# A buffer of its own for the fourth head output at the fourth place, and one left-over product moved, in a recurrent-memory transformer kernel

## The chip, the cores and the metric

The kernel runs on one core of a Trainium2 chip. Times are device microseconds (us) of one launch. A core has a matrix engine (PE in the profile; PEld is its weight load), a vector engine (DVE), a scalar engine (ACT), GpSimd (POOL), and SyncE (SP), which here only issues transfers (DMA). Each engine works through its own list in order and waits on semaphores that others raise.

## The reference

The input `x` has 2048 rows of 640. It is cut into 64 segments of 32 rows. A memory of 8 rows is put in front of each segment; attention with 32 heads of 192 runs over these 40 rows; its first 8 output rows are the memory of the next segment. So segment s+1 can't begin before the output product of segment s.

```python
for s in range(n_seg):                      # 64 segments, one after the other
    xs = x[:, s * seg_len:(s + 1) * seg_len, :].copy()
    h = jnp.concatenate([mem, xs], axis=1)  # 8 + 32 rows
    q = jnp.einsum('btd,dhe->bhte', h, Wq)
    k = jnp.einsum('btd,dhe->bhte', h, Wk)
    v = jnp.einsum('btd,dhe->bhte', h, Wv)
    scores = jnp.einsum('bhqe,bhke->bhqk', q, k) * scale
    scores = jnp.where(mask[None, None], scores, -1000000000.0)
    p = _softmax(scores, axis=-1)
    o = jnp.einsum('bhqk,bhke->bhqe', p, v)
    o = jnp.einsum('bhte,hed->btd', o, Wo)
    mem = o[:, :M, :].copy()                # M = 8
    outs.append(o[:, M:, :])
```

The result is mixed with a gated feed-forward block of the same `x` by a sigmoid gate, row by row. The feed-forward block is done once, ahead of the segments.

## The kernel before

**Layout of the work.** After the feed-forward block, `segment(s)` is recorded 64 times. The 32 heads are four *octets* of eight heads; the places of the four octets in a segment are called i = 0 to 3. Segments go in groups of four, and the *place* of a segment is q = s % 4, so there are places 0, 1, 2 and 3 (place 3 is the "fourth place" of the change). Of each segment's 32 rows, 24 are done with the memory rows in the segment itself. The other 8 are the *left rows*: four segments' left rows make 32 rows, and their Q, K and V products are done together, ahead of time. Only place 3 finishes the left rows' attention output: there the output product runs over 64 rows (40 of the segment, 24 left rows of the three segments ahead) and is a function of its own, `wo_both`; places 0 to 2 use `wo_part`.

**The order.** The order of the steps in a segment is a table written by hand: `PROG` for places 0 and 2, `PROG1` (the same but for one step) for place 1, `PROG3` for place 3. Each engine's list follows the table; a recording layer (`_Sched`) adds the waits from the regions that each step reads and writes. The steps:

- `("g", n, k)`: product of 128 of the 640 inputs for group n of Q, K or V of some octet (L1134, and L226 where the stationary operand is kept). The last k of a group is followed by the copy of the product out of PSUM: L1155 for Q and K, L1158 for V, both on ACT.
- `tq`, `tk`: DVE turns Q and K (L1172). `sc`: scores (L1183 to L1198 on PE). `ex`: softmax. `pt`: the probabilities are turned on PE (L1245, L1250).
- `("pv", i)`: probabilities times V of octet i, the *head outputs* (L1278 and L1280 on PE), written to SBUF by ACT (L1300 or L1310) and DVE (L1304 or L1315). At place 3 POOL also puts the left rows' head outputs beside them (L1292).
- `("wo", i, h)`: half h of octet i's output product. Place 3: L1372, 12 matmuls for a half, gathered in one PSUM bank. Places 0 to 2: L1328, and L1354 for octet i = 3.
- `("lf", q, u, k)`: step k of the left rows' Q and K product of the next group, done at place q only (L926 and L226). `le` takes it out (L1400, L1402).
- `("vb", k)`: at place 3, step k of the left rows' V product for the next group, five steps of four matmuls (L967). Nothing in its own segment reads it.

**The end of a segment at place 3.** After the last `wo`, DVE and ACT copy the memory rows out of PSUM (L1561, L1564), DVE turns them into the next segment's input (L1572, two pieces), and `("g", 0, 0)` of the next segment starts on the first piece. DVE then adds the segment's rows to the output (L1083, L1431).

**Buffers.** At place 3 the head outputs of every octet go into `U3`, one buffer of 4 x 3 x 64 values per partition. So `pv` of an octet can be written only after both halves of `wo` of the octet ahead have read it. At places 0 to 2 there are two buffers, and octet i = 3 is written in two halves with regions of their own.

**Weights.** Most of the weights stay in SBUF. 16 pieces share their space with another piece; after such a piece is used, SP loads its partner into the space in the same segment (L631). At place 3 three pieces of Wo are loaded so after `("wo", 0, 0)` and `("wo", 0, 1)` and used in `("wo", 3, 0)` and `("wo", 3, 1)`, in the order in which they are loaded.

Of the kernel before, what the change touches and what calls it, by code (L numbers as in the profile page):

```python
# [238 lines left out]
def _build(nc, A_x, A_mem0, A_Wq, A_Wk, A_Wv, A_Wo, seg_len, w_gate, w_up, w_down,  # L239
           gate_w, out, opts=None):  # L240
# [9 lines left out]
    DJ = Dm // 4  # L250
    NT = H // 2
    NPAIR = NT // 2
    NOCT = NT // 4
# [4 lines left out]
    R = L + M  # L258
# [15 lines left out]
    S_ = _Sched(nc)  # L274
# [18 lines left out]
    wsB = {}  # L293
# [43 lines left out]
    ps = nc.alloc_psum_tensor("ps", [128, 8, 512], F32)  # L337
# [3 lines left out]
    o = wsA_base - wsB_total  # L341
    assert o == w_cap
    wsB_off = {}
# [4 lines left out]
    o = wsA_base  # L348
# [4 lines left out]
    o = ffn_base  # L353
# [73 lines left out]
    U3 = bview(wsB_off["uT"], 1536).rearrange("p (t c r) -> p t c r", c=3, r=64)  # L427
    r_U3 = sreg(wsB_off["uT"], 1536)
    r_U3p = [[sreg(wsB_off["uT"] + x + 4 * i, 4) for x in (0, UB)] for i in range(3)]
    st_f = [[fview(wsA_off["stats"] + (2 * b + i) * 16, 16) for i in (0, 0, 1)] for b in range(2)]  # L430
    r_st = [sreg(wsA_off["stats"] + 32 * b, 32) for b in range(2)]
    uTl = bview(wsB_off["uTl"], NCH * XA * 2).rearrange("p (c t) -> p c t", t=XA)
# [85 lines left out]
    def piece_view(key, o):  # L518
        if key[0] == 3:
# [17 lines left out]
    PROG3 = [("g", 0, 0), ("g", 0, 1), ("g", 0, 2), ("g", 0, 3), ("g", 0, 4), ("tq", 0), ("g", 1, 0), ("tk", 0),  # L537
# [58 lines left out]
    o = 0  # L596
# [496 lines left out]
    LB = 4  # L1093
# [15 lines left out]
    def apx(ap, dims):  # L1109
        return bass.AP(ap.tensor, ap.offset, [list(ap.ap[0])] + [list(d) for d in dims])  # L1110
# [155 lines left out]
    def pv_oct(s, o):  # L1266
# [20 lines left out]
        S_.add("pe", fns, reads=[r_v[o % NVB], r_vl[oc], r_PT], writes=[r_ps[A]] + ([r_ps[B]] if B != A else []), name="PVa s%d o%d" % (s, o))  # L1287
        na = 2 if o in USPLIT else 3
        q = s % 4
        if q == 3:  # L1290
            u, ru = U3, r_U3p
            S_.add("pool", lambda e: e.tensor_copy(  # L1292
                out=U3.rearrange("p t c r -> p (t c) r")[:, :, R:64], in_=uTl[:, 12 * oc:12 * oc + 12, :]),
                reads=[r_uTl[oc]], writes=r_U3p[2], name="U3l s%d o%d" % (s, o))
        if o == NOCT - 2 and s + 1 < NSEG:
            ek_copy(s, (3,))
        if o == NOCT - 1 and q < 3:
            assert na == 2 and o % NUB == 1 and WOP == 4
            for h in ((0, 1), (1, 0))[s % 2]:
                S_.add("act", lambda e, h=h: e.activation(  # L1300
                    out=apx(u[:, 2 * h, 0, :], [[R, 2], [3 * R, 2], [1, R]]),
                    in_=ps[:, A, 0:2 * W].rearrange("p (c t r) -> p c t r", t=4, r=R)[:, :, 2 * h:2 * h + 2], func=ACTF.Copy),
                    reads=[r_ps[A]], writes=[r_uThp[h][0]], name="uT evac s%d o%d" % (s, o))
                S_.add("dve", lambda e, h=h: e.tensor_copy(  # L1304
                    out=u[:, 2 * h:2 * h + 2, 2, 0:R],
                    in_=ps[:, B, 2 * W:3 * W].rearrange("p (t r) -> p t r", r=R)[:, 2 * h:2 * h + 2]),
                    reads=[r_ps[B]], writes=[r_uThp[h][1]], name="uT mid s%d o%d" % (s, o))
        else:
            rs = R if q < 3 else 64
            S_.add("act", lambda e: e.activation(  # L1310
                out=apx(u[:, 0, 0, :], [[rs, na], [3 * rs, 4], [1, R]]),
                in_=ps[:, A, 0:na * W].rearrange("p (c t r) -> p c t r", t=4, r=R), func=ACTF.Copy),
                reads=[r_ps[A]], writes=ru[0] if na == 2 else ru[0] + ru[1], name="uT evac s%d o%d" % (s, o))
            if na == 2:
                S_.add("dve", lambda e: e.tensor_copy(out=u[:, :, 2, 0:R], in_=ps[:, B, 2 * W:3 * W].rearrange("p (t r) -> p t r", r=R)),  # L1315
                       reads=[r_ps[B]], writes=ru[1], name="uT mid s%d o%d" % (s, o))
# [51 lines left out]
    def wo_both(s, item):  # L1368
        for p in wo_pairs(s, item):
            g_, rg_ = piece(s, (3, p))  # L1370
            for c in range(3):
                S_.add("pe", [lambda e, i=i, g_=g_, c=c, p=p: e.matmul(  # L1372
                    ps[64 * i:64 * i + 64, LB, 0:2 * DJ], U3[:, p % 4, c, :], g_[:, c, 2 * DJ * i:2 * DJ * (i + 1)],
                    start=(p == NWP - 1 and c == 0), stop=(p == 0 and c == 2), tile_position=(0, 64 * i),
                    skip_group_check=True) for i in range(2)],
                    reads=[rg_, r_U3], writes=[r_ps[LB]], name="Wb s%d p%d" % (s, p))

    late_at = ("g", 1, KT - 1)
    r_lsth = [sreg(lst_off[3] + 768 * m, 768) for m in range(2)]
# [1 line left out]
    for x, prog in enumerate(PROGS):  # L1381
        at = prog.index
        g_end = {mi: at(("g", n, KT - 1)) for n, ms in enumerate(GROUPS) for mi in ms}
        assert g_end[(2, 1)] < at(("wo", 0, 0))
        assert at(("sc", 2)) < at(("pv", 1))
        assert all(at(("wo", i, 1)) < at(("pv", i + (1 if x == 3 else 2))) for i in range(NOCT - (1 if x == 3 else 2)))
# [279 lines left out]
```

## Time and profile before

| | |
|---|---|
| median of 3 runs | 1659.49 us (1658.9 to 1665.99) |
| profiled execution, own time | 1669.24 us |
| its span, first to last instruction | 1667.5 us |
| granted PE clock, mean | 0.996 |
| busy share of the span: PE, PEld | 94%, 47% |
| busy share: DVE, ACT, POOL | 60%, 47%, 33% |
| DMA: read and written | 473.25 MB, 21.09 MB |

A row of a timeline gives the start (us from the span's start), how long the row lasted, the engine, the line, and in brackets how long the engine stood idle before it and what ended that wait. A row "A <- B: total, times, longest" of the waits is idle time of engine A that B ended. Matmuls are pipelined and their ends are modelled, so starts are compared with starts where it matters.

### The profile page before, as it was taken

How to read it: one execution, taken by the hardware profiler on the slowest of the kernel's cores; microseconds unless marked ns; L12 is line 12 of the kernel's file. 1: busy time of each engine (PE TensorE's matmuls, PEld its weight loads, DVE VectorE, ACT ScalarE, POOL GpSimd, SP SyncE). 2: the span in 40 equal slices, each digit the busy share in tenths (PEclk: the TensorE clock that was granted, in tenths of full speed). 3: DMA queues.
4: the chain of work that ended last, by engine and by line, in shares of the span. 5: the costliest groups of instructions: out<-in, count | busy, mean ns of one | idle time of the engine just before them, and what ended most of it. 6: DMA issues, size and time to landing. Idle time of an engine off the chain costs nothing.

```text
span 1667.5 us, 75813 instructions
## 1 busy us (share of the span) xinstructions
PE 1566.5 (94%) x37107; PEld 779.2 (47%) x28147; DVE 1000.1 (60%) x3023; ACT 785.5 (47%) x1874; POOL 549.9 (33%) x1609
## 2 busy tenths in 40 slices
PE   9999899999999999999999999999999999999986
PEld 4444345444444445444455444454444454444533
DVE  6453566656566666666565666566665656656653
ACT  2222454545555454545455554455454555545442
POOL 1110233333333333333333333333333333333332
PEclk9999999999999999999999999999999999999999
DMA  9915899888889898988889898889888898888984
GB/s 297 340 43 160 323 321 330 301 282 310 324 317 325 300 319 290 334 306 311 303 305 343 315 327 289 303 315 340 308 302 310 308 336 311 307 297 308 324 312 179
DMA packets 275415, 499.28 MB, mean 299 GB/s; under 512 B 121119, under 2 KB 136327, under 8 KB 275079
## 3 DMA queue, kind: packets, MB, share of 16 engines
q1 hardware_dynamic: 271000, 491.30, 84.2%
q8 instruction: 255, 4.18, 1.0%
q10 hardware_dynamic: 4079, 3.14, 0.6%
q14 instruction: 81, 0.66, 0.1%
HBM read 473.25 MB, written 21.09 MB: 296 GB/s over the span
## 4 chain that ended last, share of the span: by engine, by line
PE 71%; DMA 17%; DVE 6%; ACT 3%; issue 3%; SPq 1%; POOL 0%; DVEq 0%; ACTq 0%; POOLq 0%
PE ps L1134 19%; PE ps L226 17%; DMA arena<-in_A_Wv_dram 9%; PE ps L1372 7%; DMA arena<-in_A_Wo_dram 6%; PE ps L1328 5%; PE ps L1278 3%; PE ps L835 3%; PE ps L832 3%; PE ps L1354 2%; PE ps L1183 2%; PE ps L926 2%; PE ps L858 2%; PE ps L1191 1%; DMA arena<-in_A_Wk_dram 1%
## 5 line engine op out<-in xcount | busy, mean ns | idle before, releaser
L1134 PE MATMUL ps<-arena 128*32 128x384 bf16 x8640 | 645.6, 328 | 28.0 <-DVE arena L1572 11.6
L226 PE MATMUL ps<-arena 128*32 128x384 bf16 x8960 | 639.7, 326 | 2.7 <-ACT arena L1155 1.2
L1134 PEld LDWEIGHTS ps<-arena 128*32 128x32 bf16 x8640 | 231.9, 96 | 399.2 <-issue 258.9
L1172 DVE STREAM_TRANSPOSE arena<-arena 128x384 bf16<-128x384 bf16 x512 | 273.6, 559 | 70.5 <-ACT arena L1155 69.3
L1155 ACT ACTIVATE arena<-ps 128x384 bf16<-128x384 f32 x512 | 230.4, 493 | 99.0 <-PE ps L1134 93.8
L1328 PE MATMUL ps<-arena 128*32 128x320 bf16 x3456 | 184.4, 300 | 16.2 <-issue 11.1
L1175 POOL COPY arena<-arena 64x160 bf16<-64x160 bf16 x256 | 81.9, 320 | 334.3 <-DVE arena L1172 332.8
L1210 DVE TENSOR_REDUCE arena<-ps 104x4 f32<-104x160 f32 x256 | 82.9, 324 | 162.3 <-PE ps L1198 162.0
L1158 ACT ACTIVATE arena<-ps 128x384 bf16<-128x384 f32 x256 | 124.9, 488 | 88.2 <-PE ps L1134 88.2
L1263 ACT ACTIVATE arena<-ps 128x448 bf16<-128x448 f32 x192 | 104.4, 544 | 125.3 <-PE ps L1250 125.3
L1222 ACT ACTIVATE ps<-ps 104x160 f32<-104x160 f32 x256 | 74.8, 292 | 177.0 <-DVE ps L1212 175.2
L1310 ACT ACTIVATE arena<-ps 128x480 bf16<-128x480 f32 (+1 forms) x208 | 116.7, 561 | 87.4 <-PE ps L1280 86.1
L1008 POOL COPY arena<-arena 128x96 bf16<-128x96 bf16 x256 | 70.2, 274 | 246.7 <-PE ps L1198 174.4
L1224 DVE TENSOR_REDUCE arena<-ps 104x4 f32<-104x160 f32 x256 | 82.9, 324 | 83.8 <-ACT ps L1222 82.4
L1372 PE MATMUL ps<-arena 128*64 128x320 bf16 x1536 | 122.6, 307 | 0.5 <-ACT arena L1310 0.5
L1278 PE MATMUL ps<-arena 128*64 128x160 bf16 x1536 | 116.9, 240 | 5.6 <-ACT arena L1155 3.4
L1328 PEld LDWEIGHTS ps<-arena 128*32 128x32 bf16 x3456 | 89.6, 96 | 62.2 <-issue 19.1
L926 PE MATMUL ps<-arena 128*32 128x384 bf16 x1280 | 109.6, 328 | 1.1 <-issue 0.8
L1280 PE MATMUL ps<-arena 128*64 128x64 bf16 x1536 | 103.7, 193 | 2.3 <-issue 1.9
L1400 ACT ACTIVATE arena<-ps 128x384 bf16<-128x384 f32 x120 | 57.3, 490 | 101.2 <-PE ps L926 48.9
L1318 POOL COPY arena<-arena 128x96 bf16<-128x96 bf16 x192 | 51.7, 270 | 159.8 <-ACT arena L1300 88.7
L1278 PEld LDWEIGHTS ps<-arena 128*64 128x64 bf16 x1536 | 81.2, 109 | 37.6 <-ACT arena L1158 14.4
(102 smaller groups left out, 2362.6 us busy)
## 6 DMA issues: line engine op xcount, KB each, us to landing
arena<-in_A_Wk_dram SPq DMA_DIRECT2D x335, 384.0 KB, 6.5
arena<-in_A_Wv_dram SPq DMA_DIRECT2D x335, 384.0 KB, 8.7
arena<-in_A_Wo_dram SPq DMA_DIRECT2D x205, 480.0 KB, 6.0
arena<-in_A_Wq_dram SPq DMA_DIRECT2D x209, 384.0 KB, 5.5
arena<-left_qk_scratch SPq DMA_DIRECT2D x126, 96.0 KB
left_qk_scratch<-arena SPq DMA_DIRECT2D x49, 192.0 KB, 5.4
left_qk_scratch<-arena SPq DMA_DIRECT2D x30, 96.0 KB, 5.5
ffn_b_scratch<-arena ACTq DMA_DIRECT2D x16, 160.0 KB, 4.1
```

The source lines that it names most:

```text
L226: return e.add_instruction(mybir.InstMatmult(name=nm, start_tensor_calc=like["start"], stop_tensor_calc=stop, tile_size=(128, 32), tile_po ...
L926: fns.append(lambda e, outp=outp, rhs=rhs, j=j: e.matmul(outp, lhs, rhs, start=(k == 0), stop=(k == KT - 1), tile_position=(0, 32 * j)))
L1134: fns.append(lambda e, outp=outp, rhs=rhs, j=j: e.matmul(outp, lhs, rhs, start=(k == 0), stop=(k == KT - 1), tile_position=(0, 32 * j)))
L1155: S_.add("act", lambda e, m=m, bk=bk: e.activation(out=rows_sb[m], in_=ps[:, bk, 0:384], func=ACTF.Copy), reads=[r_ps[bk]], writes=[r_rows ...
L1158: S_.add("act", lambda e, i=i, bk=bk: e.activation(out=v_sb[i % NVB].rearrange("p (c n) -> p c n", c=3), in_=ps[:, bk, 0:384].rearrange("p ...
L1172: S_.add("dve", lambda e: e.transpose(out=dst[:, :, 0:L], in_=rows_sb[m].rearrange("p (c r) -> p c r", r=L)), reads=[r_rows[m]], writes=[r ...
L1263: S_.add("act", lambda e: e.activation(out=PT, in_=ps[:, bank, 0:PTW + 128], func=ACTF.Copy), reads=[r_ps[bank]], writes=[r_PT], name="pT ...
L1278: return [lambda e: e.matmul(full, v[:, e0:e0 + 64], PTm[:, i], start=True, stop=False, tile_position=(0, 64 * i), skip_group_check=True), ...
L1280: lambda e: e.matmul(part, vl[:, e0:e0 + 64], PTl[:, i], start=False, stop=True, tile_position=(0, 64 * i), skip_group_check=True)]
L1310: S_.add("act", lambda e: e.activation(out=apx(u[:, 0, 0, :], [[rs, na], [3 * rs, 4], [1, R]]), in_=ps[:, A, 0:na * W].rearrange("p (c t r ...
L1328: fns.append(lambda e, i=i, t=t, j=j, gv=gv: e.matmul(ps[32 * j:32 * j + 32, bank, 0:2 * DJ].rearrange("p (h n) -> p h n", h=2), lhs2[i], ...
L1372: S_.add("pe", [lambda e, i=i, g_=g_, c=c, p=p: e.matmul(ps[64 * i:64 * i + 64, LB, 0:2 * DJ], U3[:, p % 4, c, :], g_[:, c, 2 * DJ * i:2 * ...
```

## The change

At place 3, octet i = 3 gets buffers of its own: `U3h`, two halves laid over Q and over the probabilities, which are free by then. It is written in two halves, as at places 0 to 2. `PROG3` has another order at its end. In `PROG` (and so in `PROG1`) the step `("lf", 1, 1, 2)`, done at place 1 only, goes from ahead of `("pt", 2)` to behind `("pv", 3)`.

```diff
+    U3h = [bview(wsB_off[nm], 768).rearrange("p (t c r) -> p t c r", c=3, r=64) for nm in ("Q", "p")]
+    r_U3h = [sreg(wsB_off[nm], 768) for nm in ("Q", "p")]
...
-            ("g", 4, 3), ("le", 1, 0, 1), ("g", 4, 4), ("g", 5, 0), ("g", 5, 1), ("lf", 1, 1, 2), ("pt", 2),
+            ("g", 4, 3), ("le", 1, 0, 1), ("g", 4, 4), ("g", 5, 0), ("g", 5, 1), ("pt", 2), ("wo", 0, 1), ("tk", 3),
...
+            ("wo", 2, 0), ("pt", 3), ("wo", 2, 1), ("pv", 3), ("lf", 1, 1, 2), ("lf", 2, 1, 2), ("lf", 0, 1, 1),
...
-            ("g", 5, 4), ("wo", 2, 0), ("wo", 2, 1), ("pv", 3), ("vb", 0), ("vb", 1), ("vb", 2), ("wo", 3, 0),
-            ("wo", 3, 1), ("vb", 3), ("vb", 4)]
+            ("g", 5, 4), ("wo", 2, 0), ("pv", 3), ("wo", 2, 1), ("wo", 3, 0), ("wo", 3, 1), ("vb", 0), ("vb", 1),
+            ("vb", 2), ("vb", 3), ("vb", 4)]
...
-        if q == 3:
+        if q == 3 and o < NOCT - 1:
             u, ru = U3, r_U3p
...
+        if q == 3 and o == NOCT - 1:
+            for h in ((0, 1), (1, 0))[s % 2]:
+                S_.add("pool", lambda e, h=h: e.tensor_copy(
+                    out=U3h[h].rearrange("p t c r -> p (t c) r")[:, :, R:64], in_=uTl[:, 12 * oc + 6 * h:12 * oc + 6 * h + 6, :]),
+                    reads=[r_uTl[oc]], writes=r_U3hp[h][2], name="U3l s%d o%d" % (s, o))
...
-        if o == NOCT - 1 and q < 3:
+        if o == NOCT - 1:
             assert na == 2 and o % NUB == 1 and WOP == 4
+            uh, rh, rs = ([u[:, 2 * h:2 * h + 2] for h in range(2)], [[[x] for x in y] for y in r_uThp], R) if q < 3 else (U3h, r_U3hp, 64)
...
+            u, ru = (U3h[p % 4 // 2][:, p % 2], r_U3h[p % 4 // 2]) if item[1] == NOCT - 1 else (U3[:, p % 4], r_U3)
...
-                    reads=[rg_, r_U3], writes=[r_ps[LB]], name="Wb s%d p%d" % (s, p))
+                    reads=[rg_, ru], writes=[r_ps[LB]], name="Wb s%d p%d" % (s, p))
```

Lines move down in the changed file: L967 is L971 there, L1134 is L1138, L1278 is L1282, L1280 is L1284, L1354 is L1364, L1372 is L1383.

PE at the end of a segment at place 3, before: the output products of octets 1 and 2 end (L1372 x24 is both halves of octet 2), then the head outputs of octet 3 (L1278, L1280), then three steps of the left V product (L967).

```order
L1134 MATMUL ps<-arena 32x384 x4
L1372 MATMUL ps<-arena 64x320 x24
L1278 MATMUL ps<-arena 64x160 x2
L1280 MATMUL ps<-arena 64x4x16 x2
L1278 MATMUL ps<-arena 64x160 x2
L1280 MATMUL ps<-arena 64x4x16 x2
L1278 MATMUL ps<-arena 64x160 x2
L1280 MATMUL ps<-arena 64x4x16 x2
L967 MATMUL ps<-arena 32x384 x12
L1372 MATMUL ps<-arena 64x320 x24
L967 MATMUL ps<-arena 32x384 x8
L1134 MATMUL ps<-arena 32x384 x4
```

The same place on PE in the changed program, up to the next segment's first product (the last row):

```order
L1138 MATMUL ps<-arena 32x384 x4
L1383 MATMUL ps<-arena 64x320 x12
L1282 MATMUL ps<-arena 64x160 x2
L1284 MATMUL ps<-arena 64x4x16 x2
L1282 MATMUL ps<-arena 64x160 x2
L1284 MATMUL ps<-arena 64x4x16 x2
L1282 MATMUL ps<-arena 64x160 x2
L1284 MATMUL ps<-arena 64x4x16 x2
L1383 MATMUL ps<-arena 64x320 x36
L971 MATMUL ps<-arena 32x384 x20
L1138 MATMUL ps<-arena 32x384 x4
```

The head outputs stand one half of an output product (12 matmuls) earlier, that half stands behind them, and all five steps of the left V product stand behind the last output product.

PE at place 1, before, from the last head outputs of octet 3 to the output product of octet 3:

```order
L1278 MATMUL ps<-arena 64x160 x2
L1280 MATMUL ps<-arena 64x4x16 x2
L1354 MATMUL ps<-arena 32x160 x48
L926 MATMUL ps<-arena 32x384 x4
L226 MATMUL ps<-arena 32x384 x4
```

The same place in the changed program; L930 and L226 in the third and fourth row are the moved step:

```order
L1282 MATMUL ps<-arena 64x160 x2
L1284 MATMUL ps<-arena 64x4x16 x2
L930 MATMUL ps<-arena 32x384 x4
L226 MATMUL ps<-arena 32x384 x4
L1364 MATMUL ps<-arena 32x160 x48
L930 MATMUL ps<-arena 32x384 x4
L226 MATMUL ps<-arena 32x384 x4
```

These eight matmuls stood ahead of `("pt", 2)` (L1245) before. On ACT and DVE the one copy of octet 3's head outputs at place 3 (L1310, L1315) becomes two copies of half the size each, on POOL L1292 does too; SP's list is the same in both programs.

More of the change, by code (lines that the diff above doesn't have):

```diff
@@ L429, in _build @@
     r_U3p = [[sreg(wsB_off["uT"] + x + 4 * i, 4) for x in (0, UB)] for i in range(3)]
+    U3h = [bview(wsB_off[nm], 768).rearrange("p (t c r) -> p t c r", c=3, r=64) for nm in ("Q", "p")]
+    r_U3h = [sreg(wsB_off[nm], 768) for nm in ("Q", "p")]
+    r_U3hp = [[[sreg(wsB_off[nm] + x + 4 * i, 4) for x in xs_] for i in range(3)] for nm, xs_ in (("Q", (0, 8)), ("p", (0, 256, 512)))]
+    assert wsB["Q"] >= 768 and wsB_off["p"] + 768 <= wsB_off["K"]
     st_f = [[fview(wsA_off["stats"] + (2 * b + i) * 16, 16) for i in (0, 0, 1)] for b in range(2)]
@@ L1294, in pv_oct @@
                 reads=[r_uTl[oc]], writes=r_U3p[2], name="U3l s%d o%d" % (s, o))
+        if q == 3 and o == NOCT - 1:
[3 more added lines that the diff above has]
+                    reads=[r_uTl[oc]], writes=r_U3hp[h][2], name="U3l s%d o%d" % (s, o))
         if o == NOCT - 2 and s + 1 < NSEG:
             ek_copy(s, (3,))
-        if o == NOCT - 1 and q < 3:
+        if o == NOCT - 1:
             assert na == 2 and o % NUB == 1 and WOP == 4
+            uh, rh, rs = ([u[:, 2 * h:2 * h + 2] for h in range(2)], [[[x] for x in y] for y in r_uThp], R) if q < 3 else (U3h, r_U3hp, 64)
             for h in ((0, 1), (1, 0))[s % 2]:
                 S_.add("act", lambda e, h=h: e.activation(
-                    out=apx(u[:, 2 * h, 0, :], [[R, 2], [3 * R, 2], [1, R]]),
+                    out=apx(uh[h][:, 0, 0, :], [[rs, 2], [3 * rs, 2], [1, R]]),
                     in_=ps[:, A, 0:2 * W].rearrange("p (c t r) -> p c t r", t=4, r=R)[:, :, 2 * h:2 * h + 2], func=ACTF.Copy),
-                    reads=[r_ps[A]], writes=[r_uThp[h][0]], name="uT evac s%d o%d" % (s, o))
+                    reads=[r_ps[A]], writes=rh[h][0], name="uT evac s%d o%d" % (s, o))
                 S_.add("dve", lambda e, h=h: e.tensor_copy(
-                    out=u[:, 2 * h:2 * h + 2, 2, 0:R],
+                    out=uh[h][:, :, 2, 0:R],
                     in_=ps[:, B, 2 * W:3 * W].rearrange("p (t r) -> p t r", r=R)[:, 2 * h:2 * h + 2]),
-                    reads=[r_ps[B]], writes=[r_uThp[h][1]], name="uT mid s%d o%d" % (s, o))
+                    reads=[r_ps[B]], writes=rh[h][1], name="uT mid s%d o%d" % (s, o))
         else:
@@ L1370, in wo_both @@
             g_, rg_ = piece(s, (3, p))
+            u, ru = (U3h[p % 4 // 2][:, p % 2], r_U3h[p % 4 // 2]) if item[1] == NOCT - 1 else (U3[:, p % 4], r_U3)
             for c in range(3):
-                S_.add("pe", [lambda e, i=i, g_=g_, c=c, p=p: e.matmul(
-                    ps[64 * i:64 * i + 64, LB, 0:2 * DJ], U3[:, p % 4, c, :], g_[:, c, 2 * DJ * i:2 * DJ * (i + 1)],
+                S_.add("pe", [lambda e, i=i, g_=g_, c=c, p=p, u=u: e.matmul(
+                    ps[64 * i:64 * i + 64, LB, 0:2 * DJ], u[:, c, :], g_[:, c, 2 * DJ * i:2 * DJ * (i + 1)],
                     start=(p == NWP - 1 and c == 0), stop=(p == 0 and c == 2), tile_position=(0, 64 * i),
                     skip_group_check=True) for i in range(2)],
-                    reads=[rg_, r_U3], writes=[r_ps[LB]], name="Wb s%d p%d" % (s, p))
+                    reads=[rg_, ru], writes=[r_ps[LB]], name="Wb s%d p%d" % (s, p))
     late_at = ("g", 1, KT - 1)
@@ L1385, in _build @@
         assert at(("sc", 2)) < at(("pv", 1))
-        assert all(at(("wo", i, 1)) < at(("pv", i + (1 if x == 3 else 2))) for i in range(NOCT - (1 if x == 3 else 2)))
+        assert all(at(("wo", i, 1)) < at(("pv", i + (1 if x == 3 else 2))) for i in range(NOCT - 2))
         n_wos.append(at([item for item in prog if item[0] not in ("lf", "le", "vb")][-1]))
```

9 rows, old and new, of the table PROG are left out of this document.

## The prediction

> **What bounds the kernel now.** I read the page first, for the span, then PE's waits, then the timeline of one segment's end at place 3 and one at place 1, then the landings of the transfers there.
>
> ```profile
> span 1667.5 us, 75813 instructions
> ```
>
> ```profile
> PE ps L1134 <- DVE arena L1572: 11.6, 18, 0.7
> PE ps L1328 <- issue: 11.1, 17, 1.5
> PE ps L1134 <- DMA arena<-in_A_Wv_dram: 8.8, 23, 0.7
> PE ps L1198 <- POOL arena L1292: 7.2, 1, 7.2
> PE ps L1354 <- DMA arena<-in_A_Wo_dram: 6.9, 15, 0.9
> PE ps L1354 <- DVE arena L1304: 6.0, 14, 0.4
> ```
>
> These are PE's own waits, longest first. PE is the bound: these six rows come to 51.6 us of the 1667.5, and all but one are small stops that come back segment after segment. The first row is the one that the change aims at: the next segment's first product waits for the turned memory rows (L1572). The last row is the wait for the head outputs of octet 3 at places 0 to 2. The first and the last of those at the ends of place 3, of 15 that I count in the timeline:
>
> ```profile
> 271.00 0.35 PE L1134 MATMUL ps<-arena 128*32 128x384 bf16 x4 [0.67 <-DVE arena L1572]
> ...
> 1562.19 0.35 PE L1134 MATMUL ps<-arena 128*32 128x384 bf16 x4 [0.63 <-DVE arena L1572]
> ```
>
> So 15 of the 18 waits are at place 3, 0.62 to 0.67 us each. PE at such an end:
>
> ```profile
> 820.93 1.82 PE L1372 MATMUL ps<-arena 128*64 128x320 bf16 x24
> 822.59 0.23 PE L1278 MATMUL ps<-arena 128*64 128x160 bf16 x2
> ...
> 822.98 0.94 PE L967 MATMUL ps<-arena 128*32 128x384 bf16 x12
> 823.85 1.82 PE L1372 MATMUL ps<-arena 128*64 128x320 bf16 x24
> 825.61 0.51 PE L967 MATMUL ps<-arena 128*32 128x384 bf16 x8
> 826.74 0.35 PE L1134 MATMUL ps<-arena 128*32 128x384 bf16 x4 [0.62 <-DVE arena L1572]
> ```
>
> By starts, PE has no other stop here: 24 matmuls of L1372 take 1.66 us (822.59 - 820.93), the head outputs 0.39, three steps of the left V product 0.87, or 0.29 a step, the last output product 1.76. Then come two steps, 0.58, to 826.19, and PE stands until 826.74.
>
> What ACT and DVE do meanwhile:
>
> ```profile
> 821.19 0.48 ACT L1158 ACTIVATE arena<-ps 128x384 bf16<-128x384 f32 x1
> 823.09 0.44 ACT L1310 ACTIVATE arena<-ps 128x320 bf16<-128x320 f32 x1 [1.42 <-PE ps L1280]
> ```
>
> ```profile
> 823.10 0.33 DVE L1315 CAST arena<-ps 128x160 bf16<-128x160 f32 x1 [1.89 <-PE ps L1280]
> 825.72 0.66 DVE L1561 CAST arena<-ps 32x160 bf16<-32x160 f32 x2 [2.30 <-PE ps L1372]
> 826.43 0.58 DVE L1572 STREAM_TRANSPOSE arena<-arena 128x64 bf16<-128x64 bf16 x2
> ```
>
> From the last output product's end by starts (825.61) to the next segment's first product there are 1.13 us of copy and turn. Only two steps of the left V product, 0.58 us, lie beside them.
>
> **The change part by part.**
>
> *All five steps behind the last output product.* They take 5 x 0.29 = 1.45 us, more than the 1.13 us of the chain. So the chain is covered with 0.32 us to spare, and PE goes on at once: 826.19 in place of 826.74, 0.55 us won. The work is the same, only the stop is gone. 15 x 0.55 = **8.25 us**. What is late next is PE itself.
>
> *Half an output product behind the head outputs.* The three steps gave the copies of the head outputs 0.87 us of cover; they needed 0.44 (L1310). The half of `wo` that stands there now takes 1.66 / 2 = 0.83 us, so it hides them too. The halved copies let the first pair start no later. POOL's part (L1292) no longer waits for that half of `wo` to have read the shared buffer, so it can start earlier, and the gate's steps on POOL that follow it with it: nothing, since nobody waits for them sooner. In the last segment there are no left steps, and PE waits for the copy:
>
> ```profile
> 1661.38 1.82 PE L1372 MATMUL ps<-arena 128*64 128x320 bf16 x24 [0.53 <-ACT arena L1310]
> ```
>
> That wait goes: **0.5 us**.
>
> *Head outputs one half earlier.* They need V of octet 3, which ACT takes out at 821.19 + 0.48 = 821.67. The cover was 1.66 us from 820.93; now it is 0.83, and PE arrives at 821.76, 0.09 us behind ACT. A wait is bounded from below by none, and from above by half of V's copy, 0.24 us, if ACT comes a little later than here. I take 0.05, near the lower end, since the order of the two in this row is the right one: 15 x 0.05 = **0.75 us** lost, between 0 and 3.6. The Trainium skill (*TensorE: Matmul & The Clock Gate*, "Architectural detail: the array is 16× 32×32, not 1× 128×128") says that PE can pull a weight load ahead of matmuls in flight. By it nothing would be lost with V ready 0.09 us ahead, and the sum would be 0.75 us better; no run here shows such a short margin.
>
> *Pieces of Wo needed earlier.* The last output product starts 0.87 us earlier, at 820.93 + 0.83 + 0.39 + 0.83 = 822.98 in place of 823.85, and its third loaded piece is used by the last 6 of 24 matmuls, 1.25 us in: at 824.23. Issue and landing of that piece here, and at the last such segment:
>
> ```profile
> 816.68 0.33 SPq L631 DMA_DIRECT2D arena<-in_A_Wo_dram  x1
> ```
>
> ```profile
> arena<-in_A_Wo_dram SPq DMA_DIRECT2D x1, 480.0 KB, 7.0
> ```
>
> ```profile
> 1552.11 0.33 SPq L631 DMA_DIRECT2D arena<-in_A_Wo_dram  x1
> ```
>
> ```profile
> arena<-in_A_Wo_dram SPq DMA_DIRECT2D x1, 480.0 KB, 7.8
> ```
>
> Here it lands at 823.7, half a microsecond ahead. In the other segment the use falls at 1562.19 - (826.74 - 824.23) = 1559.68, and it lands at 1559.9, 0.2 us late. Of 15 segments I find five late by the same reckoning, by 0.15 to 0.36 us, about **1.2 us** lost; the ends are 0 and 15 x 0.36 = 5.4. I take 1.2 since it is counted in the landings themselves. Nothing new is queued on SP.
>
> *The left product at place 1.* Eight matmuls go from ahead of `pt` 2 to behind `pv` 3:
>
> ```profile
> 773.86 0.54 DVE L1172 STREAM_TRANSPOSE arena<-arena 128x384 bf16<-128x384 bf16 x1
> 774.09 0.25 PE L1183 MATMUL ps<-arena 128*40 128x160 bf16 x2
> ...
> 774.45 0.28 PE L1191 MATMUL ps<-arena 128*40 128x40 bf16 x8
> ...
> 778.54 0.20 PE L1280 MATMUL ps<-arena 128*64 128x64 bf16 x2
> ...
> 779.17 1.01 PE L1354 MATMUL ps<-arena 128*32 128x160 bf16 x48 [0.44 <-DVE arena L1304]
> ```
>
> Two rows of place 2, where a left step already stands behind `pv` 3:
>
> ```profile
> 800.50 0.10 PEld L926 LDWEIGHTS ps<-arena 128*32 128x32 bf16 x4
> ...
> 801.06 0.53 PE L1354 MATMUL ps<-arena 128*32 128x160 bf16 x15
> ```
>
> Behind `pv` 3 there is room: 779.17 - 778.54 = 0.63 us, of which 0.44 idle, and at place 2 eight left matmuls fit into 0.56 us ahead of L1354. So the addition costs nothing; its Q half now reads the copy of the weights that POOL makes at `pv` 2, which place 0's step behind `pv` 3 does already. But the removal brings little: the scores of octet 3 (L1191, 774.45) start 0.05 us after DVE has turned K (773.86 + 0.54 = 774.40), and that DVE row does not depend on the moved step. PE would come earlier and wait longer. Only in the few place 1 segments that a late transfer holds up ahead of the scores is PE the later one, and a piece of Wo is asked for a little sooner. I take **0.4 us** won; the ends are 0 and 16 x 0.44 = 7.0, if all of the idle time paid.
>
> *Sum:* 8.25 + 0.5 + 0.4 - 0.75 - 1.2 = 7.2 us. The profiled execution took 1669.24 us (span 1667.5), so it would take 1662.0. The median of the runs, 1659.49, is 9.75 us below it; I take the same difference from it: 1652.3 us, 0.43% less.
>
> **The rivals.**
>
> *Code loading takes the freed time (slower).* PE idles for "issue" 17 times at L1328, 11.1 us, 0.65 us each, in places 0 to 2: no semaphore ends these. Place 3's product is L1372, and it isn't in such a row. If PE, which now runs through without a pause at the end of place 3, meets one such stop there in each round, 15 x 0.65 = 9.8 us come against 7.2: 1662.1 us, and slower from 0.5 us a round on. Against it: the same instructions in nearly the same number.
>
> ```profile
> q8 instruction: 255, 4.18, 1.0%
> ```
>
> The Trainium skill (*Runtime: NRT & Kernel Launch*, "Instruction fetch mechanics") says that code comes in blocks of 16 KiB by a DMA queue of its own, and that crossing a block is mostly hidden; by it this rival costs nothing. The blocks agree (4.18 MB / 255 = 16.4 KB); the 0.65 us stops are not hidden, if they are these.
>
> *Transfers hold it (same).* If Wo comes late at all 15 ends as at the worst, 5.4 us go in place of 1.2: 1656.5; if transfers set the pace altogether, nothing is won: 1659.5. Against it, the end of place 3, where the transfers stand still:
>
> ```profile
> 825.60:826.80 1.20, 0.58 (x14) 0.18 (x12) 0.96 (x4) 1.03 (x3) 0.16 (x1) 1.00 0.00 0
> ```
>
> The last two columns are the DMA share and GB/s: zero.
>
> *Place 1 pays as well (faster).* If the eight matmuls' time, 0.33 us, is won in each of 16 segments: 5.3 - 0.4 = 4.9 us more, 1647.4. Against it stands the K row above.
>
> **How the numbers follow.** The forecast has 0.63, code loading 0.12, transfers 0.13, place 1 0.08, anything else 0.04. About 0.5%, 8.3 us, is what a measurement of this kernel can tell from no change: the line is at 1651.2. The forecast lies 1.1 us short of it, and its own range (no V wait and no late Wo: 1650.3; both twice as large: 1654.2; the three runs themselves differ by 7 us) crosses it; I give a little under half of it, 0.29, and place 1 to faster: 0.37. Slower by over 0.5% takes code loading at over twice its mean: 0.07. The rest is 0.56. The range reaches from place 1 with some of the waits gone, 1646, to code loading, 1662.
>
> **What would show it.** Right: no row of L1138 <- L1572 at the ends of place 3, so at most three are left; a segment at place 3 shorter by 0.5 us; at place 1 L1364 <- DVE gone and a longer wait of the scores for K. Wrong: rows of L1383 <- DMA of Wo over 3 us in sum, L1282 <- ACT at V's copy over 0.1 us each, or issue stops at L971 or L1383.

## The result, and the profile after

The changed kernel takes 1650.86 us (median of 9 runs) against 1663.14 us for the kernel before, run beside it on the same chip. One of the nine runs took 2115.92 us at a granted clock of 0.654; without it the median is 1648.49 us and the ratio 0.991, 95% interval 0.9884 to 0.9935. So it is 0.9% faster, some 15 us (10.8 to 19.3), where 7.2 us were forecast. The time lies in the predicted range and 1.4 to 3.8 us under the predicted one, but that closeness is partly luck: the gain was twice the forecast, and the kernel before also ran 3.65 us longer here than in the three runs that the prediction started from.

The profile of after is that of a second run of the same kernel (`as_changed` below: own time 1647.81 us, granted clock 0.998). From its page, the span, and PE's own waits (us in total, times, longest):

```profile
span 1646.1 us, 75845 instructions
```

```profile
PE ps L1282 <- ACT arena L1159: 3.4, 15, 0.2
PE ps L1195 <- DVE arena L1176: 3.3, 14, 0.3
PE ps L1138 <- DVE arena L1583: 2.5, 6, 0.7
...
PE ps L1364 <- DVE arena L1314: 0.9, 2, 0.4
...
PE ps L1383 <- DMA arena<-in_A_Wo_dram: 0.3, 2, 0.2
PE ps L1383 <- issue: 0.3, 1, 0.3
```

The row that the change aims at, the next segment's first product behind the turned memory rows, fell from 11.6 us in 18 waits to 2.5 in 6. That is 9.1 us, less than the time fell. PE's timeline says where the rest came from. The first row is the start of a segment at place 3, the last the start of the next segment:

```profile
789.29 0.35 PE L1138 MATMUL ps<-arena 128*32 128x384 bf16 x4
...
806.64 1.01 PE L1383 MATMUL ps<-arena 128*64 128x320 bf16 x12
807.48 0.24 PE L1282 MATMUL ps<-arena 128*64 128x160 bf16 x2
...
807.78 2.62 PE L1383 MATMUL ps<-arena 128*64 128x320 bf16 x36
810.33 1.00 PE L971 MATMUL ps<-arena 128*32 128x384 bf16 x20
811.46 0.35 PE L1138 MATMUL ps<-arena 128*32 128x384 bf16 x4
```

The start of the same segment in the kernel before (its end, 826.74, stands in the prediction):

```profile
803.58 0.35 PE L1134 MATMUL ps<-arena 128*32 128x384 bf16 x4
```

The segment takes 22.17 us (811.46 - 789.29) where it took 23.16 (826.74 - 803.58): 0.99 us less. Both are the shortest of their 15 segments at place 3. Now two things are to be read here. From the end of the last output product by starts (the first L971 behind it) to the next segment there are 811.46 - 810.33 = **1.13 us, just as before** (826.74 - 825.61); over all 15 ends it is 1.13 to 1.18 us in both kernels. And the five left V steps do not fill that time: four of them pass between the first and the last start of their row, (1.00 - 0.34) / 4 = 0.165 us a step, five take 0.83, and PE stands for 0.30 us. It is no longer in the list of waits as a large row, but it is still there.

What ACT and DVE do meanwhile, first ACT and then DVE:

```profile
806.90 0.48 ACT L1162 ACTIVATE arena<-ps 128x384 bf16<-128x384 f32 x1
807.99 0.50 ACT L1310 ACTIVATE arena<-ps 128x160 bf16<-128x160 f32 x2 [0.60 <-PE ps L1284]
810.44 0.61 ACT L1575 ACTIVATE arena<-ps 32x160 bf16<-32x160 f32 x2 [1.95 <-PE ps L1383]
```

```profile
810.44 0.66 DVE L1572 CAST arena<-ps 32x160 bf16<-32x160 f32 x2 [2.06 <-PE ps L1383]
811.16 0.58 DVE L1583 STREAM_TRANSPOSE arena<-arena 128x64 bf16<-128x64 bf16 x2
```

V is out of PSUM at 807.38 (806.90 + 0.48), 0.10 us ahead of the head outputs that need it (807.48). The copy and the turn of the memory rows take as long as before.

### The profile page after: what moved, and what is told of

Its sections match the earlier page's. It is cut to its first block, busy times and chain, and to the rows that moved or that the text cites. A ratio compares the mean times of both kernels' runs of the same rounds, so it can differ in the third digit from the quotient of the medians.

```text
span 2114.2 us, 75845 instructions
## 1 busy us (share of the span) xinstructions
PE 2098.0 (99%) x37107; PEld 958.1 (45%) x28147; DVE 1005.8 (48%) x3039; ACT 792.9 (38%) x1890; POOL 553.3 (26%) x1625
## 4 chain that ended last, share of the span: by engine, by line
PE 99%; DMA 0%; DVE 0%; SPq 0%; POOL 0%; ACT 0%; issue 0%; ACTq 0%; POOLq 0%; DVEq 0%
PE ps L226 26%; PE ps L1138 25%; PE ps L1338 9%; PE ps L1383 8%; PE ps L1282 4%; PE ps L930 4%; PE ps L839 4%; PE ps L836 4%; PE ps L862 3%; PE ps L1364 3%; PE ps L1187 2%; PE ps L1284 2%; PE ps L234 1%; PE ps L1195 1%; PE ps L971 1%; PE ps L1254 1%
## 5 line engine op out<-in xcount | busy, mean ns | idle before, releaser
L226 PE MATMUL ps<-arena 128*32 128x384 bf16 x8960 | 887.8, 430 | 0.4 <-ACT arena L1159 0.4
L1138 PE MATMUL ps<-arena 128*32 128x384 bf16 x8640 | 857.5, 420 | 2.0 <-DVE arena L1583 2.0
L1138 PEld LDWEIGHTS ps<-arena 128*32 128x32 bf16 x8640 | 303.3, 117 | 525.3 <-issue 379.7
L1159 ACT ACTIVATE arena<-ps 128x384 bf16<-128x384 f32 x512 | 230.0, 491 | 160.1 <-PE ps L1138 160.1
L1338 PE MATMUL ps<-arena 128*32 128x320 bf16 x3456 | 241.0, 404 | 0.0
L1012 POOL COPY arena<-arena 128x96 bf16<-128x96 bf16 x256 | 70.2, 274 | 475.3 <-PE ps L1202 311.4
L1162 ACT ACTIVATE arena<-ps 128x384 bf16<-128x384 f32 x256 | 125.2, 489 | 128.1 <-PE ps L1138 127.5
L1383 PE MATMUL ps<-arena 128*64 128x320 bf16 x1536 | 169.6, 387 | 0.0
L1320 ACT ACTIVATE arena<-ps 128x480 bf16<-128x480 f32 x192 | 109.5, 570 | 93.8 <-PE ps L1284 85.7
L930 PE MATMUL ps<-arena 128*32 128x384 bf16 x1280 | 142.5, 408 | 0.0
L1338 PEld LDWEIGHTS ps<-arena 128*32 128x32 bf16 x3456 | 113.3, 129 | 56.9 <-ACT arena L1261 18.1
L1282 PE MATMUL ps<-arena 128*64 128x160 bf16 x1536 | 135.2, 263 | 0.0
L1284 PE MATMUL ps<-arena 128*64 128x64 bf16 x1536 | 128.6, 225 | 0.0
L1383 PEld LDWEIGHTS ps<-arena 128*64 128x64 bf16 x1536 | 93.2, 127 | 49.4 <-issue 9.6
L1282 PEld LDWEIGHTS ps<-arena 128*64 128x64 bf16 x1536 | 94.1, 126 | 42.8 <-ACT arena L1159 23.0
```

Of the source, the lines that this page charges most:

```text
L226: return e.add_instruction(mybir.InstMatmult(name=nm, start_tensor_calc=like["start"], stop_tensor_calc=stop, tile_size=(128, 32), tile_po ...
L930: fns.append(lambda e, outp=outp, rhs=rhs, j=j: e.matmul(outp, lhs, rhs, start=(k == 0), stop=(k == KT - 1), tile_position=(0, 32 * j)))
L1138: fns.append(lambda e, outp=outp, rhs=rhs, j=j: e.matmul(outp, lhs, rhs, start=(k == 0), stop=(k == KT - 1), tile_position=(0, 32 * j)))
L1159: S_.add("act", lambda e, m=m, bk=bk: e.activation(out=rows_sb[m], in_=ps[:, bk, 0:384], func=ACTF.Copy), reads=[r_ps[bk]], writes=[r_rows ...
L1162: S_.add("act", lambda e, i=i, bk=bk: e.activation(out=v_sb[i % NVB].rearrange("p (c n) -> p c n", c=3), in_=ps[:, bk, 0:384].rearrange("p ...
L1282: return [lambda e: e.matmul(full, v[:, e0:e0 + 64], PTm[:, i], start=True, stop=False, tile_position=(0, 64 * i), skip_group_check=True), ...
```

## The experiments

Two accounts stand against each other. By the **cover account**, that of the prediction, five left V steps are longer than copy and turn, so PE's work ends the segment; a step costs 0.29 us wherever it stands. By the **chain account**, copy and turn still end the segment 1.13 us behind the last output product; left V steps behind it are free, and what counts is how early that product stands.

**The changed kernel again, and its two parts.** `as_changed` is the kernel with no edit.

> The changed kernel again, for a profile at full clock. The comparison gave about 0.9% (some 14 us) less than before, where the prediction's sum was 7.2 us. By the sum (place 3's stop gone, little from place 1): 15 stops of 0.55 us gone at the ends of place 3, place 3 segments at 22.6 us in place of 23.16, place 1 segments within 0.1 us of the 23.0 of before. If place 1 pays as well: place 1 segments shorter by 0.33 us, 5 us in all. If the rest comes from elsewhere: stops for transfers or for issue at places 0 and 2 smaller than in the profile before, with places 1 and 3 as in the sum.

`place3_only` keeps the table of places 0 to 2 as it was:

```diff
-            ("g", 4, 3), ("le", 1, 0, 1), ("g", 4, 4), ("g", 5, 0), ("g", 5, 1), ("pt", 2), ("wo", 0, 1), ("tk", 3),
+            ("g", 4, 3), ("le", 1, 0, 1), ("g", 4, 4), ("g", 5, 0), ("g", 5, 1), ("lf", 1, 1, 2), ("pt", 2),
...
-            ("wo", 2, 0), ("pt", 3), ("wo", 2, 1), ("pv", 3), ("lf", 1, 1, 2), ("lf", 2, 1, 2), ("lf", 0, 1, 1),
...
+            ("wo", 1, 1), ("g", 5, 4), ("wo", 2, 0), ("pt", 3), ("wo", 2, 1), ("pv", 3), ("lf", 2, 1, 2),
```

> Only the part at place 3: buffer of its own and the other order of PROG3; the left product at place 1 stays ahead of pt 2 as before. By the prediction's sum 6.8 us less than before (8.25 + 0.5 - 0.75 - 1.2), 0.41%. If place 1 carries the missing 7 us: again 7 us, and the changed kernel 7 us below this one. If place 3 is worth more than the sum: 12 to 15 us less than before, the changed kernel within 2 us of it.

`place1_only` is the kernel before with nothing but that step moved as the change moves it.

> Only the part at place 1: the step (lf, 1, 1, 2) behind pv 3, everything at place 3 as before. By the prediction 0.4 us less than before, so no difference that can be measured; PE waits 0.33 us longer for K ahead of the scores of octet 3 and no longer for the head outputs. If place 1 pays: 5 to 7 us less (0.3 to 0.4%), with place 1 segments 0.33 to 0.44 us shorter.

Measured against before: `as_changed` 0.9919 (0.9897 to 0.9941), `place3_only` 0.9899 (0.9881 to 0.9916), `place1_only` 0.999 (0.9975 to 1.0005). The whole gain is at place 3, where the shortest segment is 22.17 us in both kernels that have its part and 23.16 us in `place1_only`. What the moved step does at place 1 can be read from PE's waits of `place1_only`:

```profile
PE ps L1191 <- DVE arena L1172: 3.7, 14, 0.3
...
PE ps L1354 <- DVE arena L1304: 0.9, 2, 0.4
```

and of `place3_only`, where the step is not moved:

```profile
PE ps L1364 <- ACT arena L1310: 6.9, 14, 0.5
```

With the step moved, the wait for the head outputs nearly goes (6.0 us in 14 waits before, 0.9 in 2 now), and a wait of the scores for K comes, 3.7 us in 14. Without it the first one stays, 6.9 us in 14. The time does not tell the two apart. In single traces the 16 segments at place 1 come to less with the step moved (363.0 us in `place1_only` against 368.6 before, 364.1 in `as_changed` against 366.1 in `place3_only`), but those at place 2 to more (362.0 against 358.6, 357.7 against 354.0).

**Three left V steps back ahead of the last output product** (`left_v_ahead`), with the rest of the change kept:

```diff
-            ("g", 5, 4), ("wo", 2, 0), ("pv", 3), ("wo", 2, 1), ("wo", 3, 0), ("wo", 3, 1), ("vb", 0), ("vb", 1),
-            ("vb", 2), ("vb", 3), ("vb", 4)]
+            ("g", 5, 4), ("wo", 2, 0), ("pv", 3), ("wo", 2, 1), ("vb", 0), ("vb", 1), ("vb", 2), ("wo", 3, 0), ("wo", 3, 1),
+            ("vb", 3), ("vb", 4)]
```

> As changed, but with the first three steps of the left V product ahead of the last output product again (behind the second half of octet 2's output product), so two steps lie behind the last output product as before. Buffer of its own and place 1 as changed. By the sum the stop of 0.55 us at the ends of place 3 is back, 15 x 0.55 = 8.25 us more than the changed kernel, and late pieces of Wo cost nothing: 7 us more than the changed kernel. If the gain at place 3 came from the head outputs standing earlier and not from the cover at the end: within 2 us of the changed kernel.

Measured: 0.9967 (0.9946 to 0.9988), shortest segment 22.89 us. The median is 9 us above that of `as_changed` (1658.82 against 1649.87), which both accounts allow; the distances decide. PE's timeline at the end of one segment at place 3, where 816.93 is the last of the three steps, cut out of the row of 816.60:

```profile
815.68 0.98 PE L1383 MATMUL ps<-arena 128*64 128x320 bf16 x12
816.60 0.67 PE L971 MATMUL ps<-arena 128*32 128x384 bf16 x12
...
816.93 0.34 PE L971 MATMUL ps<-arena 128*32 128x384 bf16 x4
817.20 1.82 PE L1383 MATMUL ps<-arena 128*64 128x320 bf16 x24
818.95 0.51 PE L971 MATMUL ps<-arena 128*32 128x384 bf16 x8
820.08 0.35 PE L1138 MATMUL ps<-arena 128*32 128x384 bf16 x4 [0.62 <-DVE arena L1583]
```

With two steps behind the product instead of five it is still 1.13 us to the next segment (820.08 - 818.95). So the 0.72 us by which the segment is longer (22.89 - 22.17) lie ahead of the end of that product. And the three steps take 0.60 us here (817.20 - 816.60), where the same three took 0.87 before.

**The kernel before's order with the buffers of the change** (`before_order_halves`): half an output product no longer stands between the head outputs and the left V steps.

```diff
-            ("g", 5, 4), ("wo", 2, 0), ("pv", 3), ("wo", 2, 1), ("wo", 3, 0), ("wo", 3, 1), ("vb", 0), ("vb", 1),
-            ("vb", 2), ("vb", 3), ("vb", 4)]
+            ("g", 5, 4), ("wo", 2, 0), ("wo", 2, 1), ("pv", 3), ("vb", 0), ("vb", 1), ("vb", 2), ("wo", 3, 0),
+            ("wo", 3, 1), ("vb", 3), ("vb", 4)]
```

> The changed kernel's buffer of its own, written in two halves, with the order of before at place 3 (place 1 as changed). Three left V steps took 0.87 us in the trace of before and 0.60 us where half an output product stands between them and the head outputs. If the 0.26 us were a hidden wait for the copies of the head outputs, halves make it shorter by 0.1 to 0.2 us: first left V step to first matmul of the last output product 0.65 to 0.75 us, place 3 segments 23.0 us in place of 23.16, 2 to 3 us less than before. If 0.29 us is what a step costs, the distance stays 0.87 us and the time that of before, less 0.5 us in the last segment.

Measured: 0.9972 (0.9946 to 0.9997), shortest segment 23.02 us. PE's timeline there; the second row, again, is a piece of the first:

```profile
812.73 0.81 PE L971 MATMUL ps<-arena 128*32 128x384 bf16 x12
...
813.20 0.34 PE L971 MATMUL ps<-arena 128*32 128x384 bf16 x2
813.47 1.82 PE L1383 MATMUL ps<-arena 128*64 128x320 bf16 x24
815.22 0.51 PE L971 MATMUL ps<-arena 128*32 128x384 bf16 x8
816.35 0.35 PE L1138 MATMUL ps<-arena 128*32 128x384 bf16 x4 [0.62 <-DVE arena L1583]
```

The three steps take 0.74 us here. Why 0.60, 0.74 and 0.87 for the same matmuls? In the kernel before, the last two matmuls of the third step carry the waits of the output product behind them:

```
L967 MATMUL ps<-arena 32x384 x10
L967 MATMUL ps<-arena 32x384 [waits e_act]
L967 MATMUL ps<-arena 32x384 [waits e_pool]
L1372 MATMUL ps<-arena 64x320 [waits e_dve]
```

The waits are for the copies of the head outputs on ACT and POOL. The timeline of the kernel before, cut so close that only those two are left:

```profile
823.58 0.34 PE L967 MATMUL ps<-arena 128*32 128x384 bf16 x2
```

They start at 823.58, 0.60 us into the row of 822.98, and ACT's copy (L1310) ended at 823.09 + 0.44 = 823.53. In `left_v_ahead` the whole third step, these two with it, starts 0.33 us into its row (816.93 - 816.60): nothing waits. So 0.27 us of the "0.87 us of work" was a wait, and the profile shows no idle time there because the matmuls ahead, which last 0.33 us each in the model, cover it. In `before_order_halves` the two start 0.47 us into the row; 0.14 us of the wait are left. The wait is 0.26 us or more in 14 of 15 segments of the kernel before, 0.14 in all 15 of `before_order_halves`. The segments fit: 23.16 - 23.02 = 0.14 and 23.16 - 22.89 = 0.27.

**One left V step ahead of the head outputs** (`left_v_one_ahead`), to give V's copy room:

```diff
-            ("g", 5, 4), ("wo", 2, 0), ("pv", 3), ("wo", 2, 1), ("wo", 3, 0), ("wo", 3, 1), ("vb", 0), ("vb", 1),
+            ("g", 5, 4), ("wo", 2, 0), ("vb", 0), ("pv", 3), ("wo", 2, 1), ("wo", 3, 0), ("wo", 3, 1), ("vb", 1),
```

> As changed, but one of the five steps of the left V product stands between the first half of octet 2's output product and the head outputs of octet 3, so four lie behind the last output product. Two theories. Cover (the prediction): a step is worth 0.29 us, four cover 1.16 us of a chain of 1.13, so nothing changes against the changed kernel (within 1 us). Chain: in the traces PE still waits for the memory rows after the change, and the last output product's last matmul stands 1.36 us ahead of the next segment in before and changed alike; the gain is that it stands earlier. Then a step ahead of it costs its full 0.17 to 0.4 us at each of 15 ends: 2.5 to 6 us more than the changed kernel.

Measured: 0.9961 (0.9935 to 0.9987), shortest segment 22.56 us, 0.39 more than with the change. PE's timeline, the end of place 3 and then a place in the segment behind it, and the first row of its waits:

```profile
817.28 0.83 PE L971 MATMUL ps<-arena 128*32 128x384 bf16 x16
818.41 0.35 PE L1138 MATMUL ps<-arena 128*32 128x384 bf16 x4 [0.30 <-DVE arena L1583]
...
824.42 0.33 PE L226 MATMUL ps<-arena 128*32 128x384 bf16 x4 [0.84 <-ACT arena L1159]
```

```profile
PE ps L226 <- ACT arena L1159: 13.9, 18, 0.9
```

Again 1.13 us (818.41 - 817.28), with four steps beside it. A step ahead of the last product costs, a step behind it is free. The time as a whole isn't a clean test of that, since the step also brought a wait of 0.84 us into place 0: the segments at place 0, without the first, are 23.6 us in the mean here and 23.3 in `as_changed`.

**The chain itself shorter** (`memory_copy_split`): ACT and DVE copy the memory rows in two parts, and the first part is turned while the second is copied. Cut to its core:

```diff
-        if q == 3:
-            for j in (0, 2, 1, 3):
...
+        def zq_part(ka, kb, i):
+            for j in ((0, 2, 1, 3), (0, 2, 3, 1))[i]:
...
+            if q == 3:
+                zq_part(ka, kb, i)
```

> As changed, and the copy of the memory rows out of PSUM at place 3 is split in two, so that the columns which the next segment's first two products need are copied and turned first. Cover theory: the chain is hidden behind five left V steps, so a shorter chain is worth nothing (within 1 us of the changed kernel). Chain theory: the distance from the last matmul of the output product to the next segment falls from 1.36 us by 0.15 to 0.25 us, 2 to 4 us less than the changed kernel, if the second piece is not late for the third product.

Measured: 0.9944 (0.9917 to 0.9971), shortest segment at place 3 22.08 us, but the segments at place 0, without the first, are 23.7 us in the mean (23.3 in `as_changed`). PE first, then DVE:

```profile
817.55 1.00 PE L971 MATMUL ps<-arena 128*32 128x384 bf16 x20
818.61 0.35 PE L1139 MATMUL ps<-arena 128*32 128x384 bf16 x4
...
819.49 0.35 PE L1139 MATMUL ps<-arena 128*32 128x384 bf16 x4
```

```profile
817.66 0.51 DVE L1574 CAST arena<-ps 32x64 bf16<-32x64 f32 x2 [2.06 <-PE ps L1384]
...
819.14 0.29 DVE L1588 STREAM_TRANSPOSE arena<-arena 128x96 bf16<-128x96 bf16 x1 [0.46 <-ACT arena L1577]
...
821.39 1.04 DVE L1177 STREAM_TRANSPOSE arena<-arena 128x384 bf16<-128x384 bf16 x2
```

The same DVE row in `as_changed`, the turn of the first Q and K:

```profile
813.69 1.04 DVE L1176 STREAM_TRANSPOSE arena<-arena 128x384 bf16<-128x384 bf16 x2
```

The chain lost only 0.07 us (818.61 - 817.55 = 1.06): two copies of 64 columns take 0.51 us on DVE, where two of 160 took 0.66. The second part's copies run on the same engines, and the second piece of turned rows, needed by the third group of products, came late: it is turned at 819.43, and that product, 0.66 us into the segment with the change, comes at 0.88 (819.49 - 818.61). DVE's list behind it slipped as well: Q and K are turned 2.78 us into the segment (821.39 - 818.61) instead of 2.23 (813.69 - 811.46). What was gained at place 3 was lost again, and more, in the next segment.

**A wait for ACT at `pv` 0.** The kernel as changed waits 0.22 us there, 15 times. ACT and then PE of `as_changed` at one of them:

```profile
796.56 0.48 ACT L1162 ACTIVATE arena<-ps 128x384 bf16<-128x384 f32 x1
796.93 0.50 ACT L1159 ACTIVATE arena<-ps 128x384 bf16<-128x384 f32 x1
```

```profile
797.48 0.26 PE L1282 MATMUL ps<-arena 128*64 128x160 bf16 x2 [0.22 <-ACT arena L1159]
```

One of the expectations below calls it a wait for V's copy. The rows say otherwise: V's copy (L1162) ended at 797.04, and PE starts 0.05 us behind the end of the next one (L1159, 797.43), a copy of Q or K. Why the head outputs wait for that one was not tried; the edits only put one more step ahead of them. `copy_split_and_pv0` is `memory_copy_split` with the step `("g", 3, 1)` moved ahead of `pv` 0; `changed_pv0_later` is the changed kernel with it, and `place3_pv0_later` is `place3_only` with it:

```diff
-            ("pv", 0), ("g", 3, 1), ("tq", 2), ("tk", 2), ("g", 3, 2), ("g", 3, 3), ("ex", 1), ("g", 3, 4),
+            ("g", 3, 1), ("pv", 0), ("tq", 2), ("tk", 2), ("g", 3, 2), ("g", 3, 3), ("ex", 1), ("g", 3, 4),
```

> The split copy of the run before this, and at place 3 the head outputs of octet 0 behind one more step of the third group, since PE waits 0.22 us for ACT ahead of them in every segment at place 3. By the chain theory 15 x 0.22 = 3.3 us less than the split copy alone; by any theory in which transfers or code loading set the pace of place 3, no difference.

> The kernel as changed, but at place 3 the step ("g", 3, 1) goes from behind ("pv", 0) to ahead of it, with V's copy as before (in one piece on ACT). In the kernel as changed PE waits 0.22 us at pv 0 of place 3 for that copy, 15 times, 3.4 us. Chain theory (the memory copy ends place 3, so work done earlier in the segment only counts if nothing else holds PE up between): the row L1282 <- ACT L1159 goes, and place 3 is shorter by 0.22 us, 3.4 us in all, so about 1645 us where the kernel as changed gave 1649.9. Rival (the wait comes back at the next step that needs the softmax or the scores): the row goes, another takes its place, and the time is as changed.

> The part of the change at place 3 alone (the left product at place 1 stays ahead of pt 2), and the step ("g", 3, 1) of place 3 goes from behind ("pv", 0) to ahead of it. If the 0.22 us wait at pv 0 is PE's own loss, place 3 is 0.22 us shorter than with the place-3 part alone (22.17 us at its shortest becomes 21.95) and the time is 3 us under its 1648.3. If something later in the segment takes the wait over, the shortest segment stays at 22.17.

Measured: 0.9951 (0.9924 to 0.9978), 0.9929 (0.9908 to 0.995) and 0.9917 (0.99 to 0.9934). None is told apart from the kernel that it was made from. The row L1282 <- ACT is gone from the waits, and the shortest segment of place 3 fell to 21.95, 21.98 and 21.99 us; but over all 15 nothing is shown to be won: in `changed_pv0_later` the mean is 22.46 us against 22.56 in `as_changed`, the median 22.50 against 22.44. PE's timeline of `changed_pv0_later` shows what comes next:

```profile
809.71 2.21 PE L1383 MATMUL ps<-arena 128*64 128x320 bf16 x30
812.10 0.60 PE L1383 MATMUL ps<-arena 128*64 128x320 bf16 x6 [0.18 <-DMA arena<-in_A_Wo_dram]
```

The third piece of Wo is late, as it is at six of the 15 ends in this kernel (1.6 us in all) and in `as_changed` (1.5), at eight in `place3_pv0_later` (2.2) and at four in `place3_only` (1.3).

## Why the prediction was right or wrong

**The step that failed is the size of a left V step.** The prediction read "three steps of the left V product 0.87, or 0.29 a step" from row starts, and from it "5 x 0.29 = 1.45 us, more than the 1.13 us of the chain". A step takes 0.165 us. From there both halves of the main term went wrong:

| 0.99 us per segment of place 3 | us |
|---|---|
| three steps of 0.165 now lie beside the chain | 0.50 |
| the wait for the copies inside the 0.87 us | 0.26 |
| two changes fewer between products over 64 and over 32 rows, 0.10 each | 0.20 |
| rest | 0.03 |

The third term can be read from starts, the same at all 15 ends. Within L1383 the pairs of matmuls start 0.13 us apart, but the first left V matmul starts 0.23 behind the last pair; one left V step starts 0.16 behind another, but in `left_v_ahead`, where nothing waits, L1383 starts 0.26 behind the last step. Head outputs and output product both work on 64 rows, and the step from one to the other has no such price (0.13 and 0.03). The change leaves out two of three such changes. The two runs that put them back agree: three steps and two changes come to 0.70 us where `left_v_ahead` lost 0.72, one step and two changes to 0.37 where `left_v_one_ahead` lost 0.39. Why such a change costs time no run shows.

So the stop at the end is not "gone": it was 0.80 us by starts (1.13 less two steps) and is now 0.30. The prediction counted 15 x 0.55 = 8.25 us for it; the undisturbed segments say 15 x 0.99 = 14.9. (All 15, disturbed ones too, took 352.6 us in the profile before and 338.4 in `as_changed`.)

**What ends the segment was wrong with it.** "What is late next is PE itself" doesn't hold: copy and turn end the segment in every kernel here, 1.13 to 1.18 us behind the last output product with two, four or five steps beside them (1.03 to 1.06 with the copy in two parts). The change gains because this product stands earlier. The forecast "no row of L1138 <- L1572 at the ends of place 3" (it is L1583 in the changed file) is half right: the rows shrank to 0.13 to 0.18 us, most of them too small for the list.

**The wait for V (0.75 us lost)** did not come. In all 15 segments V is ready 0.10 us ahead, about the predicted 0.09, and the head outputs start 0.13 us behind the last pair of matmuls ahead of them, the pace of those pairs themselves. Here the Trainium skill (*TensorE: Matmul & The Clock Gate*, "Architectural detail: the array is 16× 32×32, not 1× 128×128"), by which nothing would be lost, gave the better value; that a pulled weight load is the reason no run shows. The row L1282 <- ACT of 3.4 us is the wait at `pv` 0, which stood in the kernel before with the same size.

**The late Wo (1.2 us lost)** was right in kind and near in size: 1.5 us, at six of 15 ends. (Done again from the landings before, its reckoning gives four late ends, 0.13 to 0.32 us, and not five.) The list of waits shows only 0.3 us of it, since the rest, like the wait above, lies inside rows. One end with a listed wait and one without, PE's timeline of `as_changed`:

```profile
267.15 0.60 PE L1383 MATMUL ps<-arena 128*64 128x320 bf16 x6 [0.15 <-DMA arena<-in_A_Wo_dram]
...
1268.55 2.88 PE L1383 MATMUL ps<-arena 128*64 128x320 bf16 x36
```

The second row is 36 matmuls in 2.88 us where the undisturbed row of 807.78 takes 2.62.

**The last segment (0.5 us won)** was undersized. PE before, the row of octet 2's output product and a wait that the prediction passed over:

```profile
1658.27 1.82 PE L1372 MATMUL ps<-arena 128*64 128x320 bf16 x24
...
1660.64 0.22 PE L1280 MATMUL ps<-arena 128*64 128x64 bf16 x1 [0.26 <-POOL arena L1292]
```

and after:

```profile
1638.02 1.00 PE L1383 MATMUL ps<-arena 128*64 128x320 bf16 x12
...
1639.16 2.62 PE L1383 MATMUL ps<-arena 128*64 128x320 bf16 x36
```

From the start of octet 2's product to that of octet 3's there were 1661.38 - 1658.27 = 3.11 us; now there are 1639.16 + 0.85 - 1638.02 = 1.99. So 1.1 us were won: POOL's wait went as well as ACT's.

**Place 1 (0.4 us won)** was right in its mechanism. The K row still sets the scores of octet 3, DVE and then PE of `as_changed`:

```profile
760.48 0.53 DVE L1176 STREAM_TRANSPOSE arena<-arena 128x384 bf16<-128x384 bf16 x1
```

```profile
761.07 0.28 PE L1195 MATMUL ps<-arena 128*40 128x40 bf16 x8 [0.22 <-DVE arena L1176]
```

PE comes earlier and waits 0.22 us for it (3.3 us in 14 waits in the list), and `place1_only` can't be told from before (gain 0.1%, interval -0.05 to 0.25%). The rival that place 1 pays 4.9 us more is outside that interval.

**The other rivals.** Code loading would have stopped PE at L971 or L1383. The list has one such stop of 0.3 us; by starts, two of the 15 rows of L1383 hold a stop at a matmul that carries no wait, 0.7 us in all, and no row of L971 does. That is far from one in each round; what those two are no run shows. Transfers held up six ends, 1.5 us, not all.

With the measured terms, and the 0.4 us of place 1 that no run can resolve, the sum is 14.9 + 1.1 + 0.4 - 1.5 = 14.9 us, against 15.0 measured; with an interval of 10.8 to 19.3 us, so close an agreement is luck. The chances put a change within 0.5% first, at 0.56, because the forecast of 7.2 us lay just short of that line of 8.3 us; the corrected terms lie far beyond it, where the prediction gave 0.37.

## What to carry to other kernels

Measure a group's own pace by what its members take where nothing can hold them up (here 0.165 us a step in a run of five), not by the distance of row starts, before putting it against a chain that it is to cover: a wait that sits on a matmul late in a row is shown as busy time. Where a chain of copies ends a stage, ask of each step not whether it covers the chain but on which side of the chain's start it stands; work in front of the start costs its full length (here more: 0.39 us for a step of 0.165), work behind it is free as long as it is shorter than the chain (here 0.83 of 1.13 us). And before shortening such a chain, follow its second half into the next stage, where it may be the first half of another.

## What the runs showed of the hardware

- A wait of 0.26 us at the last two matmuls of a row left no idle time in the profile, since the modelled 0.33 us of the matmuls ahead covered it. The Trainium skill (*Perfetto Trace Analysis*, "Tensor Engine Instruction (MATMUL, LD_WEIGHTS)") says that the end of such an instruction is estimated and not observed; the trace agrees, and so a short stop of PE, here 0.26 us, has to be looked for between starts.
- Head outputs whose V was ready 0.10 us ahead started at the pace of the matmuls in front of them, in all 15 segments.
- A change between products over 64 and over 32 rows cost PE about 0.10 us by starts, at all 15 ends of place 3.
- One step moved ahead of the head outputs of place 3 made PE wait 0.84 us for a copy in the next segment, 6 us later, 15 times. That another PSUM bank is chosen there, since the left V step takes its own bank earlier, was only argued.
